# Inputs of four units loaded at once, moves of the first block on ScalarE's queue, and idle products on TensorE: one change to a fused attention and two-layer kernel

## The chip, the cores and the metric

One core of a Trainium2 chip runs the whole program. The metric is the device time of one execution in microseconds (us). One execution was profiled; its span (first to last instruction) and its own time are given below.

## What is computed

The reference, cut to what matters (B, H, S, D = 4, 8, 768, 48; 3072 tokens of 384 numbers; the hidden layers are 2048 wide):

```python
f = 1.0 / (1.0 + np.exp(-f_logit))
for t in range(S):
    state = f[:, :, t, :, None] * state + np.einsum('bhd,bhe->bhde', k[:, :, t], v[:, :, t])
    y[:, :, t] = np.einsum('bhd,bhde->bhe', q[:, :, t], state)
x = y as (3072, 384)
h = x @ w_in;  x = softplus(h) @ w_out            # first layer
h = x @ w_in2; x = (a clipped square of h) @ w_out2   # second layer
```

The weights of the layers arrive as 64-bit floats, everything else as 32-bit floats.

## The kernel before

**Units.** The recurrence is cut into 24 units (4 batches by 6 chunks of 128 time steps); a unit has all 8 heads. `pre(n)` makes a unit ready. It loads four inputs (`t_f`, `t_k`, `t_q` of 256 KB each and `vz` of 192 KB, L536 ff.). ScalarE takes an exponential (L559) and VectorE or ScalarE adds one (L413 or L415); GpSimd writes the first column of `cap` (L563); VectorE runs the scan that gives the running product `ip` (L565). The keys are multiplied by `ip` (L557), ScalarE takes a logarithm and an exponential (L571, L572), and three more passes of VectorE (L557, L575, L557) make the inverse `pt` exact and multiply the queries by it. TensorE transposes the keys (L586) and a copy brings them to `ks`.

`main(n)` then does the unit's products: keys by queries into two banks (`amm`, L605), two masks on VectorE (L611), the update of the state (`dmm`, L631, with L660 and L663 on VectorE), and the output (`ymm`, L646 and, from the second chunk on, L652). ScalarE copies the output from its bank to `ys` (L675), and six transfers per unit (`moves`, issued at L424) put it into the layout that the layers read: `xr2` for the first block, `xhl` for the later ones.

**Layers.** Tokens are taken in six blocks of 512 per layer, and each block in 16 steps of 128 hidden columns. A step is a product `hmm` (L728), the activation on ScalarE and VectorE (L758 to L773), and a product `second` (L807 in the first block, L802 to L804 later). The first block needs four units, since 4 x 128 = 512 tokens. It uses 32-bit products with weights just converted from 64 bits (three VectorE passes, L473, L476, L478, then a transfer `wl<-wa`); chunks 2 to 15 of these weights are converted while the first block runs.

**What sets the order.** The program writes the operations down in one order; `Order.schedule` (a planner with a cost in ns for each operation) then fixes the order on every engine. Engines run their own list strictly in that order and wait on semaphores. Every transfer takes the next of eight completion semaphores in turn, and is issued only when the transfer that had this semaphore before it has landed. Before, all transfers are issued by SP, in one list. Around the start the text writes `pre(0)`, `pre(1)`, the conversion of two weight chunks, `main(0)`, `main(1)`, and then `attention()`, which interleaves `pre(2)`, `main(2)` with `pre(3)`, and so on. There are three buffers of each input, one `ip` and one `pt`, so the fourth unit's inputs go into the first unit's buffers:

```python
t_f = buf("t_f", [P, NA, P], 3, pool=attp)
t_k = buf("t_k", [P, NA, P], NQ, pool=attp)      # NQ = 3
ip = attp.tile([P, NA, P], F32, name="ip")
pt = attp.tile([P, NA, P], F32, name="pt")
```

In orders below, t_f_138 to 140, t_k_141 to 143, t_q_144 to 146 and vz_135 to 137 are the three buffers of each input; stg, wa, wl are the stages of a weight chunk (staged, converted, stored); bank_69 to 76 are the eight banks; ys_156 and 157 the two output buffers; xr_124 is `xr2`; g_127 to 129 are `g_0`, the three buffers of the first block's activation, tu_121 is `t_u`, ip_147 and 148 the two buffers of `ip`.

Of the kernel before, what the change touches and what calls it, by code (L numbers as in the profile page):

```python
# [30 lines left out]
NQ = 3  # L31
# [283 lines left out]
def attn_moe_moe2_kernel(ctx: ExitStack, tc: tile.TileContext, q, k, v, f_logit,  # L315
# [46 lines left out]
    bank = buf("bank", [P, 512], 8, pool=psum)  # L362

# [26 lines left out]
    ip = attp.tile([P, NA, P], F32, name="ip")  # L390
    pt = attp.tile([P, NA, P], F32, name="pt")
# [6 lines left out]

    nc.scalar.preload_act_table_set("natural_log_exp_and_others")
# [122 lines left out]

    abank = [0]
# [11 lines left out]

    def load(n):  # L536


        b, c = divmod(n, NCH)
        t = slice(c * P, c * P + P)  # L540
        dma(t_f[n % 3], f_logit[b, :, :, t], [], [("t_f", n % 3)], 262e3)
        dma(t_k[n % NQ], k[b, :, :, t], [], [("t_k", n % NQ)], 262e3)
        dma(t_q[n % NQ], q[b, :, :, t], [], [("t_q", n % NQ)], 262e3)
        dma(vz[n % NQ], v[b, t], [], [("vz", n % NQ)], 197e3)
        attn_keys.update([("t_f", n % 3), ("t_k", n % NQ), ("t_q", n % NQ), ("vz", n % NQ)])

    def pre(n):
        b, c = divmod(n, NCH)
        z = n % 2
        F, K, Q = t_f[n % 3], t_k[n % NQ], t_q[n % NQ]  # L550
        ktf, kk, kq = [("t_f", n % 3)], ("t_k", n % NQ), ("t_q", n % NQ)
        kip, kpt = [("ip",)], [("pt",)]
# [3 lines left out]
        def tt(o, x, y, op, reads, writes):  # L556
# [9 lines left out]
            out=ip.rearrange("p a t -> p (a t)"), data0=F.rearrange("p a t -> p (a t)"),  # L566
            data1=cap.rearrange("p a t -> p (a t)"), initial=1.0, op0=ALU.mult, op1=ALU.min), ktf + [("cap",)], kip)
        yield
        tt(K, K, ip, ALU.mult, [kk] + kip, [kk])

        ado("act", c_act(NB), lambda: nc.scalar.activation(out=pt, in_=ip, func=AF.Ln), kip, kpt)  # L571
        ado("act", c_act(NB), lambda: nc.scalar.activation(out=F, in_=pt, func=AF.Exp, scale=-1.0), kpt, ktf)  # L572
        yield
        tt(pt, ip, F, ALU.mult, kip + ktf, kpt)
        ado("dve", c_dve(NB), lambda: nc.vector.scalar_tensor_tensor(  # L575
            out=pt, in0=pt, scalar=2.0, in1=F, op0=ALU.subtract, op1=ALU.mult, reverse0=True), kpt + ktf, kpt)
        tt(Q, Q, pt, ALU.mult, [kq] + kpt, [kq])
        ado("dve", c_dve(NA), lambda: nc.vector.tensor_copy(pcall[:, n, :], pt[:, :, P - 1]), kpt, [("pcall", n)])
        yield
        if c < NCH - 1:  # L580
# [7 lines left out]
            ado("pe", 400, f, [kk], [kb])  # L588
            ado(copy_any(NA * R, lambda: ks[z], lambda: pbv, True), 0, None, [kb], [("ks", z)])
# [128 lines left out]


    O1 = [0, 1, 2]  # L720
    H1 = [3, 4]
    H2 = [3, 5, 1]
    O2 = [4, 7, 6]

# [302 lines left out]
```

## Time and profile before

| | |
|---|---|
| time, median of 3 runs (lowest, highest) | 961.5 us (961.21, 963.16) |
| the profiled execution: its own time / its span | 960.75 / 958.7 us |
| TensorE busy | 923.1 us (96%) |
| VectorE, ScalarE, GpSimd busy | 661.4, 641.0, 78.3 us |
| TensorE busy in us 0 to 10, 10 to 20, 40 to 50 of the span | 0.98, 7.00, 3.64 us |
| first block's products run on from | 49.22 us after the start |

How to read it: the profile is one execution; times in its views are us from the span's start. "Busy" is the time an engine executes; a wait is put down to what ended it. SPq is the issuing of transfers by SP, PEclk is TensorE's granted clock as a share of 2.4 GHz.

### The profile page before, as it was taken

The numbers are of one execution on the slowest core, as the hardware profiler recorded it, in microseconds if no ns is written. First come the engines' busy times: TensorE is split into PE (matmuls) and PEld (weight loads), VectorE is DVE, ScalarE is ACT, GpSimd is POOL, SyncE is SP. The second block draws the span as 40 slices with busy tenths as digits, with TensorE's granted clock in tenths as the row PEclk, the third lists the DMA queues.
The fourth block names the chain that finished last, engine by engine and source line by source line (L and its number), as shares of the span: only waits on it lengthen the run. The fifth ranks groups of instructions, "written<-read, shape, count | busy, mean of one in ns | idle before, by whom it ended". The sixth has DMA issues, their size and how long they took to land.

```text
span 958.7 us, 13366 instructions
## 1 busy us (share of the span) xinstructions
PE 923.1 (96%) x4850; PEld 715.7 (75%) x4850; DVE 661.4 (69%) x1034; ACT 641.0 (67%) x1140; POOL 78.3 (8%) x89
## 2 busy tenths in 40 slices
PE   4789998999999999999999999999999999999997
PEld 3544455887787787888887878887888888888885
DVE  5769997998777778756799995444454454544542
ACT  4256656977877787766787777878984454544443
POOL 1001111021001001001003001000010010100000
PEclk9889999999999999999999999999999999999999
DMA  7477856325312322120152356775640100100001
GB/s 215 109 228 237 251 160 204 119 65 175 114 50 75 105 71 71 47 87 17 41 171 69 121 176 181 211 202 195 204 160 1 66 0 1 66 1 1 34 0 37
DMA packets 106890, 103.98 MB, mean 108 GB/s; under 512 B 8001, under 2 KB 89921, under 8 KB 106817
## 3 DMA queue, kind: packets, MB, share of 16 engines
q1 hardware_dynamic: 106816, 103.05, 35.6%
q8 instruction: 40, 0.66, 0.3%
q14 instruction: 34, 0.27, 0.1%
HBM read 78.64 MB, written 9.44 MB: 92 GB/s over the span
## 4 chain that ended last, share of the span: by engine, by line
PE 74%; DVE 11%; DMA 5%; ACT 5%; issue 2%; SPq 2%; POOL 0%; DVEq 0%; ACTq 0%
PE bank L728 33%; PE bank L802 10%; PE bank L804 10%; PE bank L803 10%; PE bank L807 4%; PE bank L605 3%; PE bank L646 2%; SPq L424 2%; PE bank L652 2%; DMA stg<-in_moe_w_in_dram 1%; DVE tl L765 1%; DVE te L763 1%; DVE wa L478 1%; DVE tl L771 1%; PE bank L631 1%
## 5 line engine op out<-in xcount | busy, mean ns | idle before, releaser
L728 PE MATMUL bank<-xhl,wh 128*128 128x512 f32 x840 | 260.4, 391 | 0.0
L728 PEld LDWEIGHTS bank<-xhl,wh 128*128 128x128 f32 x840 | 158.5, 189 | 32.5
L728 PE MATMUL bank<-xhl,wl 128*128 128x512 f32 x420 | 168.3, 401 | 3.0 <-DVE tl L765 3.0
L802 PE MATMUL bank<-gh,wl 128*128 128x512 f32 x420 | 164.6, 392 | 1.0 <-ACT gh L419 1.0
L804 PE MATMUL bank<-gl,wh 128*128 128x512 f32 x420 | 163.9, 390 | 1.4 <-DVE gl L773 1.4
L803 PE MATMUL bank<-gh,wh 128*128 128x512 f32 x420 | 163.5, 389 | 0.0
L419 ACT CAST gh<-tl 128x512 fp32r<-128x512 f32 x176 | 108.9, 619 | 74.4 <-DVE tl L788 48.9
L788 DVE TENSOR_TENSOR tl<-bank,te 128x512 f32<-128x512 f32 x96 | 66.4, 691 | 69.8 <-ACT te L787 69.8
L790 DVE TENSOR_TENSOR gl<-tl,gh 128x512 fp32r<-128x512 f32 x96 | 67.5, 703 | 60.4 <-ACT gh L419 59.5
L758 ACT ACTIVATE te<-bank 128x512 f32<-128x512 f32 x96 | 57.0, 594 | 74.8 <-PE bank L728 74.6
L728 PEld LDWEIGHTS bank<-xhl,wl 128*128 128x128 f32 x420 | 79.2, 189 | 22.8 <-DVE tl L765 4.0
L804 PEld LDWEIGHTS bank<-gl,wh 128*128 128x128 f32 x420 | 78.8, 188 | 19.1 <-DVE gl L773 2.5
L802 PEld LDWEIGHTS bank<-gh,wl 128*128 128x128 f32 x420 | 78.8, 188 | 18.7 <-ACT gh L419 1.8
L803 PEld LDWEIGHTS bank<-gh,wh 128*128 128x128 f32 x420 | 78.9, 188 | 16.2
L783 ACT ACTIVATE te<-bank 128x512 f32<-128x512 f32 x96 | 57.1, 595 | 49.0 <-PE bank L728 48.2
L787 ACT ACTIVATE te<-te 128x512 f32<-128x512 f32 x96 | 60.5, 630 | 40.8 <-DVE te L785 40.8
L763 DVE SCALAR_TENSOR_TENSOR te<-tu,te 128x512 f32<-128x512 f32 x96 | 67.2, 700 | 24.1 <-ACT tu L415 23.8
L785 DVE TENSOR_SCALAR te<-te 128x512 f32<-128x512 f32 x96 | 45.2, 471 | 51.8 <-ACT te L783 51.8
L773 DVE TENSOR_TENSOR gl<-tl,gh 128x512 fp32r<-128x512 f32 x80 | 56.8, 709 | 21.0 <-ACT gh L419 20.6
L765 DVE SCALAR_TENSOR_TENSOR tl<-bank,tl 128x512 f32<-128x512 f32 x96 | 65.8, 685 | 2.2 <-ACT tl L761 2.1
L728 PE MATMUL bank<-xhl,wxh 128*128 128x512 f32 x216 | 66.9, 391 | 0.0
L759 ACT ACTIVATE te<-te 128x512 f32<-128x512 f32 x96 | 60.6, 632 | 2.0
(87 smaller groups left out, 1390.8 us busy)
## 6 DMA issues: line engine op xcount, KB each, us to landing
stg<-in_moe_w_out_dram SPq DMA_DIRECT2D x64, 384.0 KB, 3.9
stg<-in_moe_w_in_dram SPq DMA_DIRECT2D x32, 384.0 KB, 3.7
stg<-in_moe_w_in_dram SPq DMA_DIRECT2D x32, 288.0 KB, 4.1
t_f<-in_f_logit_dram SPq DMA_DIRECT2D x24, 256.0 KB, 3.5
t_k<-in_k_dram SPq DMA_DIRECT2D x24, 256.0 KB, 3.7
t_q<-in_q_dram SPq DMA_DIRECT2D x24, 256.0 KB, 3.8
xhl<-ys SPq DMA_DIRECT2D x80, 72.0 KB, 2.3
wl<-wa SPq DMA_DIRECT2D x14, 384.0 KB, 3.0
```

The source lines that it names most:

```text
L419: "act": (c_act(n, ps), lambda: nc.scalar.copy(o(), x()))}
L728: nc.tensor.matmul(o, l, r, start=(j == 0), stop=(j == n - 1))
L759: do("act", c_act(N), lambda: nc.scalar.activation(out=e, in_=e, func=AF.Exp, scale=-1.0), [ke], [ke])
L763: do("dve", c_dve(N), lambda: nc.vector.scalar_tensor_tensor(out=e, in0=u, scalar=-1.0, in1=e, op0=ALU.add, op1=ALU.subtract), [ku, ke], [ke])
L765: do("dve", c_dve(N), lambda: nc.vector.scalar_tensor_tensor(out=l, in0=h, scalar=0.0, in1=l, op0=ALU.max, op1=ALU.add), [kb, kl], [kl])
L783: do("act", c_act(N, True), lambda: nc.scalar.activation(out=r, in_=h, func=AF.Relu, scale=0.5, bias=0.5), [kb], [kr])
L787: do("act", c_act(N), lambda: nc.scalar.activation(out=r, in_=r, func=AF.Square), [kr], [kr])
L788: do("dve", c_dve(N), lambda: nc.vector.tensor_tensor(out=l, in0=h, in1=r, op=ALU.max), [kb, kr], [kl])
L790: do("dve", c_dve(N), lambda: nc.vector.tensor_tensor(out=gl, in0=l, in1=gh.bitcast(F32), op=ALU.subtract), [kl, kgh], [kgl])
L802: nc.tensor.matmul(o, ol, gh, start=(c == 0), stop=False)
L803: nc.tensor.matmul(o, oh, gh, start=False, stop=False)
L804: nc.tensor.matmul(o, oh, gl, start=False, stop=(c == NFC - 1))
```

## The change

1. All inputs of units 0 to 3 get places of their own: unit 3's go into buffers that the first block uses only later (`g_0` and `t_u`, by `inputs_of`). `ip` gets two buffers and `pt` is gone (the steps that used it work in place in `ip` and `t_f`). The text now writes the first four steps of `pre(0)` to `pre(3)` ahead of everything else; the last step of each and `main(0)`, `main(1)` follow the conversion of two weight chunks, and `attention()` starts with `main(2)`.
2. The six moves of a unit of the first block are issued on ScalarE's queue (`nc.scalar.dma_start`, L717) and no longer on SP's. Later blocks keep SP.
3. TensorE multiplies a zeroed 128x128 tile by itself (`keep_warm`, L532): 18 times at the very start, 5 times after the first unit's transposes, and 5 times after the keys-by-queries products of each of the first four units. Nothing reads the results; they go to a bank that the first block overwrites.

The core of the diff:

```diff
@@ -387,8 +391,7 @@
     t_f = buf("t_f", [P, NA, P], 3, pool=attp)
     t_k = buf("t_k", [P, NA, P], NQ, pool=attp)
     t_q = buf("t_q", [P, NA, P], NQ, pool=attp)
-    ip = attp.tile([P, NA, P], F32, name="ip")
-    pt = attp.tile([P, NA, P], F32, name="pt")
+    ip = buf("ip", [P, NA, P], 2, pool=attp)
     ks = buf("ks", [P, NA, R], 2, pool=attp)
     am = buf("am", [P, NA, P], 2, pool=attp)
     sst = buf("sst", [P, NA, D], 2, pool=attp)
@@ -396,6 +399,8 @@
 
     ys = buf("ys", [P, 2, NA, P], 2, pool=attp)
 
+    warm = attp.tile([P, P], F32, name="warm")
+    nc.vector.memset(warm, 0.0)
     nc.scalar.preload_act_table_set("natural_log_exp_and_others")
 
 
@@ -520,6 +525,14 @@
         attn_keys.update(writes)
         do(eng, cost, fn, reads, writes, delay)
 
+    def keep_warm(n, after=()):
+
+        def f():
+            for _ in range(n):
+                nc.tensor.matmul(bank[H1[1]][:, 0:P], warm, warm, start=True, stop=True)
+
+        do("pe", 217 * n, f, after, [("bank", H1[1])])
+
     abank = [0]
     tbank = [0]
     ndone = [0]
@@ -533,23 +546,32 @@
         abank[0] += 1
         return bank[r], ("bank", r)
 
+    def inputs_of(n):
+
+
+        if n == 3:
+            g = [x.rearrange("p (a t) -> p a t", a=NA) for x in g_0]
+            return (g[2], g[0], g[1], t_u[0][:, 0:NA * E2]), (("gh", 2), ("gh", 0), ("gh", 1), ("tu", 0))
+        i = n if n < 3 else (n - 1) % NQ
+        return (t_f[i], t_k[i], t_q[i], vz[i]), (("t_f", i), ("t_k", i), ("t_q", i), ("vz", i))
+
     def load(n):
 
 
         b, c = divmod(n, NCH)
         t = slice(c * P, c * P + P)
-        dma(t_f[n % 3], f_logit[b, :, :, t], [], [("t_f", n % 3)], 262e3)
-        dma(t_k[n % NQ], k[b, :, :, t], [], [("t_k", n % NQ)], 262e3)
-        dma(t_q[n % NQ], q[b, :, :, t], [], [("t_q", n % NQ)], 262e3)
-        dma(vz[n % NQ], v[b, t], [], [("vz", n % NQ)], 197e3)
-        attn_keys.update([("t_f", n % 3), ("t_k", n % NQ), ("t_q", n % NQ), ("vz", n % NQ)])
+        tiles, keys = inputs_of(n)
+        for o, i, key, size in zip(tiles, (f_logit[b, :, :, t], k[b, :, :, t], q[b, :, :, t], v[b, t]), keys,
+                                   (262e3, 262e3, 262e3, 197e3)):
+            dma(o, i, [], [key], size)
+        attn_keys.update(keys)
 
     def pre(n):
         b, c = divmod(n, NCH)
         z = n % 2
-        F, K, Q = t_f[n % 3], t_k[n % NQ], t_q[n % NQ]
-        ktf, kk, kq = [("t_f", n % 3)], ("t_k", n % NQ), ("t_q", n % NQ)
-        kip, kpt = [("ip",)], [("pt",)]
+        (F, K, Q, _), (kf, kk, kq, _) = inputs_of(n)
+        I = ip[z]
+        ktf, kip = [kf], [("ip", z)]
         load(n)
         yield
 
@@ -563,19 +585,19 @@
         ado("pool", 450, lambda: nc.gpsimd.tensor_scalar(
             out=cap[:, :, 0:1], in0=F[:, :, 0:1], scalar1=2.0 ** 62, scalar2=1.0, op0=ALU.min, op1=ALU.max), ktf, [("cap",)])
         ado("dve", 70 + 2.08 * NB, lambda: nc.vector.tensor_tensor_scan(
-            out=ip.rearrange("p a t -> p (a t)"), data0=F.rearrange("p a t -> p (a t)"),
+            out=I.rearrange("p a t -> p (a t)"), data0=F.rearrange("p a t -> p (a t)"),
             data1=cap.rearrange("p a t -> p (a t)"), initial=1.0, op0=ALU.mult, op1=ALU.min), ktf + [("cap",)], kip)
         yield
-        tt(K, K, ip, ALU.mult, [kk] + kip, [kk])
-
-        ado("act", c_act(NB), lambda: nc.scalar.activation(out=pt, in_=ip, func=AF.Ln), kip, kpt)
-        ado("act", c_act(NB), lambda: nc.scalar.activation(out=F, in_=pt, func=AF.Exp, scale=-1.0), kpt, ktf)
+        tt(K, K, I, ALU.mult, [kk] + kip, [kk])
+
+        ado("act", c_act(NB), lambda: nc.scalar.activation(out=F, in_=I, func=AF.Ln), kip, ktf)
+        ado("act", c_act(NB), lambda: nc.scalar.activation(out=F, in_=F, func=AF.Exp, scale=-1.0), ktf, ktf)
         yield
-        tt(pt, ip, F, ALU.mult, kip + ktf, kpt)
+        tt(I, I, F, ALU.mult, kip + ktf, kip)
         ado("dve", c_dve(NB), lambda: nc.vector.scalar_tensor_tensor(
-            out=pt, in0=pt, scalar=2.0, in1=F, op0=ALU.subtract, op1=ALU.mult, reverse0=True), kpt + ktf, kpt)
-        tt(Q, Q, pt, ALU.mult, [kq] + kpt, [kq])
-        ado("dve", c_dve(NA), lambda: nc.vector.tensor_copy(pcall[:, n, :], pt[:, :, P - 1]), kpt, [("pcall", n)])
+            out=I, in0=I, scalar=2.0, in1=F, op0=ALU.subtract, op1=ALU.mult, reverse0=True), kip + ktf, kip)
+        tt(Q, Q, I, ALU.mult, [kq] + kip, [kq])
+        ado("dve", c_dve(NA), lambda: nc.vector.tensor_copy(pcall[:, n, :], I[:, :, P - 1]), kip, [("pcall", n)])
         yield
         if c < NCH - 1:
             pb, kb = att_bank(n * P < BLOCKS1[0])
@@ -586,15 +608,16 @@
                     nc.tensor.transpose(pbv[:, a, :], K[0:R, a, :], ident[0:R, 0:R])
 
             ado("pe", 400, f, [kk], [kb])
+            if n == 0:
+                keep_warm(5, [kb])
             ado(copy_any(NA * R, lambda: ks[z], lambda: pbv, True), 0, None, [kb], [("ks", z)])
         yield
 
     def main(n):
         b, c = divmod(n, NCH)
         z = n % 2
-        kk, kq = ("t_k", n % NQ), ("t_q", n % NQ)
-        kv = [("vz", n % NQ)]
-        K, Q, V = t_k[n % NQ], t_q[n % NQ], vz[n % NQ]
+        (_, K, Q, V), (_, kk, kq, kv) = inputs_of(n)
+        kv = [kv]
         banks = [att_bank() for _ in range(2)]
 
         def amm():
@@ -604,7 +627,9 @@
                     r = slice(64 * hh, 64 * hh + D)
                     nc.tensor.matmul(banks[hh][0][:, a * P:(a + 1) * P], K[r, a, :], Q[r, a, :], start=True, stop=True)
 
-        ado("pe", 1000, amm, [kk, kq], [kp for _, kp in banks])
+        ado("pe", 1030, amm, [kk, kq], [kp for _, kp in banks])
+        if n < 4:
+            keep_warm(5, [kp for _, kp in banks])
         for hh, (pa, kp) in enumerate(banks):
             pav = pa.rearrange("p (a t) -> p a t", a=NA)
             attn_keys.update([kp, ("am", hh)])
@@ -689,7 +714,8 @@
                     o, i = xr2[dst, 0:3, sl], Y[src, 0, 0:3, :]
                 else:
                     o, i = xr2[dst, m, sl], Y[src, 0, 3, :]
-                dma(o, i, [kyh], [("x0", xs, u)], size)
+                do("act", 500, lambda o=o, i=i: nc.scalar.dma_start(out=o, in_=i), [kyh], [("x0", xs, u)],
+                   delay=1700 + size / 250)
             else:
                 if m is None:
                     for j in range(2):
@@ -703,11 +729,8 @@
 
     def attention():
         done = object()
-        p = pre(2)
-        while next(p, done) is not done:
-            yield 1
         for n in range(2, NU):
-            p = pre(n + 1) if n + 1 < NU else iter(())
+            p = pre(n + 1) if 3 < n + 1 < NU else iter(())
             m = main(n)
             while True:
                 x = next(m, done)
@@ -886,16 +905,23 @@
         t0 += N
 
     s_of = {}
-    for n in range(2):
-        for _ in pre(n):
-            pass
-        s_of[1, n] = load_w(1, n)
+
+    keep_warm(18)
+    first = [pre(n) for n in range(4)]
+    for n, p in enumerate(first):
+        for _ in range(4):
+            next(p)
+        if n < 2:
+            s_of[1, n] = load_w(1, n)
     for c in range(2):
         conv_w(1, c, s_of.pop((1, c)))
         s_of[1, c + 2] = load_w(1, c + 2)
-    for n in range(2):
-        for _ in main(n):
+    for n in range(4):
+        for _ in first[n]:
             pass
+        if n > 0 and n < 3:
+            for _ in main(n - 1):
+                pass
     agen = attention()
     pieces = [0]
 
```

**SP's list** around the first units' outputs. Before (the row "xr_124<-ys_156 48x3x128 x2" is the first two moves of unit 0):

```order
L424 DMA vz_135<-in_v_dram 128x384
L424 DMA xr_124<-ys_156 48x3x128 x2
L424 DMA stg_112<-in_moe_w_in_dram 96x3x256
L424 DMA xr_124<-ys_156 32x128 x2
L424 DMA xr_124<-ys_156 16x128 x2
L424 DMA xr_124<-ys_157 48x3x128 x2
L424 DMA xr_124<-ys_157 32x128 x2
L424 DMA xr_124<-ys_157 16x128 x2
L424 DMA stg_112<-in_moe_w_in_dram 32x3x256
L424 DMA stg_112<-in_moe_w_out_dram 128x768
L424 DMA t_f_139<-in_f_logit_dram 128x4x128
L424 DMA wl_95<-wa_125 128x384 x2
```

Now:

```order
L429 DMA g_129<-in_f_logit_dram 128x4x128
L429 DMA vz_136<-in_v_dram 128x384
L429 DMA t_q_146<-in_q_dram 128x4x128
L429 DMA g_127<-in_k_dram 128x4x128
L429 DMA vz_137<-in_v_dram 128x384
L429 DMA g_128<-in_q_dram 128x4x128
L429 DMA stg_111<-in_moe_w_out_dram 128x768
L429 DMA stg_111<-in_moe_w_in_dram 96x3x256
L429 DMA stg_111<-in_moe_w_in_dram 32x3x256
L429 DMA tu_121<-in_v_dram 128x384
L429 DMA stg_112<-in_moe_w_in_dram 96x3x256
L429 DMA stg_112<-in_moe_w_in_dram 32x3x256
```

The moves have left SP's list: weight chunk 1 (stg_112) and the next two units' inputs no longer stand behind the moves of units 0 and 1, and unit 3's inputs (g_129, g_127, g_128, tu_121) stand ahead of it.

**ScalarE's list** at the outputs of units 2 and 3 (L675 before, L700 now, ys_156 and ys_157). Before:

```order
L419 COPY ks_150<-bank_70 128x448
L675 COPY ys_156<-bank_76 112x512
L559 ACTIVATE t_f_139<-t_f_139 128x512
L415 ACTIVATE t_f_139<-t_f_139 128x512
L675 COPY ys_157<-bank_74 112x512
L419 CAST wh_79<-wl_95 128x768
L571 ACTIVATE pt<-ip 128x512
L572 ACTIVATE t_f_139<-pt 128x512
```

Now, with what each row waits for (DMAHW0 to 7 are the eight completion semaphores of transfers):

```order
L581 ACTIVATE t_f_139<-t_f_139 128x512
L420 ACTIVATE t_f_139<-t_f_139 128x512 [waits Activation_49]
L700 COPY ys_157<-bank_74 112x512 [waits DMAHW3_49,DMAHW1_49,DMAHW6_49,DVE_49,PE_49]
L593 ACTIVATE t_f_138<-ip_147 128x512 [waits DVE_49]
L717 DMA xr_124<-ys_157 48x3x128 [waits DMAHW5_49,Activation_49]
L717 DMA xr_124<-ys_157 48x3x128 [waits DMAHW6_49]
L717 DMA xr_124<-ys_157 32x128 [waits DMAHW0_49]
L717 DMA xr_124<-ys_157 32x128 [waits DMAHW1_49]
L717 DMA xr_124<-ys_157 16x128 [waits DMAHW3_49]
L717 DMA xr_124<-ys_157 16x128 [waits DMAHW4_49]
L594 ACTIVATE t_f_138<-t_f_138 128x512 [waits Activation_49]
L593 ACTIVATE t_f_139<-ip_148 128x512 [waits DVE_49]
```

Between unit 3's output copy and the next work of ScalarE now stand one logarithm of unit 4 and six issues of moves; each of the issues waits for an earlier transfer on its semaphore.

**TensorE's list** at its start, with the idle products (warm); t_k_141 are the keys of unit 0, and L656 is its state update:

```order
L532 MATMUL bank_73<-warm 128x128 x18
L608 MATMUL bank_70<-ident,t_k_141 128x112 x4
L532 MATMUL bank_73<-warm 128x128 x5
L656 MATMUL bank_76<-vz_135,ks_149 64x48
L656 MATMUL bank_76<-vz_135,ks_149 48x48
```

Before, the list began with the transposes of t_k_141.

## Rows read from the trace of the kernel before

**Rows 1.** Busy time by stretch: stretch, length, then each engine's busy us (instructions), PEclk, DMA share, GB/s.

```profile
49.00:60.00 11.00, 9.49 (x17) 4.05 (x18) 5.25 (x9) 5.69 (x9) 0.00 (x0) 0.81 0.84 239
60.00:100.00 40.00, 40.00 (x151) 18.86 (x150) 39.13 (x56) 25.90 (x43) 4.59 (x3) 1.00 0.78 238
100.00:155.00 55.00, 52.24 (x281) 26.53 (x279) 50.63 (x76) 34.42 (x59) 6.35 (x7) 1.00 0.64 187
580.00:952.00 372.00, 371.51 (x1633) 305.54 (x1631) 181.54 (x295) 228.64 (x425) 19.34 (x13) 1.00 0.27 83
```

**Rows 2.** The chain that ended last, us 39 to 61: start, us, what.

```profile
40.86 0.59 ACT ys L675
...
41.48 0.58 SPq L424
...
46.55 0.59 SPq L424
...
47.19 1.79 DMA xr<-ys
...
49.22 3.77 PE bank L728 x4
...
59.01 1.29 PE bank L728 x3
```

**Rows 3.** Timeline of TensorE, products of units 2 and 3: start, us, what, [idle before].

```profile
28.46 2.08 PE L605 MATMUL bank<-t_q,t_k 48*128 48x128 f32 x16
...
36.20 1.16 PE L605 MATMUL bank<-t_q,t_k 48*128 48x128 f32 x16
...
39.74 1.08 PE L652 MATMUL bank<-t_q,sst 48*48 48x128 f32 x16
```

**Rows 4.** Busy time by stretch, as in Rows 1: the clock's fall and rise.

```profile
43.00:44.00 1.00, 0.00 (x0) 0.00 (x0) 0.03 (x1) 0.85 (x2) 0.00 (x0) 0.50 0.69 150
53.00:54.00 1.00, 1.00 (x3) 0.43 (x3) 0.00 (x0) 0.96 (x2) 0.00 (x0) 0.88 1.05 295
```

**Rows 5.** Who held up SP's list, us 0 to 60: waiter, releaser: us in total, times, longest.

```profile
SPq L424 <- ACT pt L571: 5.4, 2, 4.7
```

**Rows 6.** The page's bandwidth by slice of 24 us.

```profile
GB/s 215 109 228 237 251 160 204 119 65 175 114 50 75 105 71 71 47 87 17 41 171 69 121 176 181 211 202 195 204 160 1 66 0 1 66 1 1 34 0 37
```

**Rows 7.** Timeline of VectorE: its first pass of a unit, and the masks of units 2 and 3.

```profile
4.78 0.43 DVE L413 TENSOR_SCALAR t_f<-t_f 128x512 f32<-128x512 f32 x1 [3.30 <-ACT t_f L559]
...
31.05 1.28 DVE L611 TENSOR_TENSOR am<-bank,mask 128x512 f32<-128x512 f32 x2
...
37.39 1.29 DVE L611 TENSOR_TENSOR am<-bank,mask 128x512 f32<-128x512 f32 x2 [1.51 <-PE bank L605]
```

**Rows 8.** Groups by line and shape, us 0 to 45, VectorE: busy us, mean ns | idle before.

```profile
L565 DVE TENSOR_TENSOR_SCAN ip<-t_f,cap 128x512 f32<-128x512 f32 x5 | 6.1, 1217 | 0.0
L611 DVE TENSOR_TENSOR am<-bank,mask 128x512 f32<-128x512 f32 x8 | 5.3, 685 | 4.0 <-PE bank L605 4.0
...
L476 DVE SCALAR_TENSOR_TENSOR wa<-stg,wa 128x384 int32<-128x384 int32 x4 | 2.2, 550 | 0.0
...
L473 DVE TENSOR_SCALAR wa<-stg 128x384 int32<-128x384 int32 x4 | 1.4, 354 | 0.1
...
L578 DVE COPY pcall<-pt 128x4 f32<-128x4 f32 x4 | 0.7, 163 | 0.0
```

**Rows 9.** The same for ScalarE.

```profile
L571 ACT ACTIVATE pt<-ip 128x512 f32<-128x512 f32 x5 | 3.2, 631 | 4.5 <-DVE pcall L578 2.5 <-DVE ip L565 2.0
```

**Rows 10.** Transfers issued in us 35 to 38.5: KB each, us from issue to landing.

```profile
stg<-in_moe_w_out_dram SPq DMA_DIRECT2D x1, 384.0 KB, 6.4
...
xr<-ys SPq DMA_DIRECT2D x1, 72.0 KB, 5.7
```

**Rows 11.** The same, us 38.5 to 48.

```profile
xr<-ys SPq DMA_DIRECT2D x4, 8.0 KB, 1.7
```

**Rows 12.** The page's section of transfers, whole execution: x count, KB each, us to landing.

```profile
stg<-in_moe_w_out_dram SPq DMA_DIRECT2D x64, 384.0 KB, 3.9
```

More of the change, by code (lines that the diff above doesn't have):

```diff
@@ L362, in attn_moe_moe2_kernel @@
     bank = buf("bank", [P, 512], 8, pool=psum)
+    O1 = [0, 1, 2]
+    H1 = [3, 4]
+    H2 = [3, 5, 1]
+    O2 = [4, 7, 6]
     xhl = const.tile([P, 2, NK, XR], F32R, name="xhl")
@@ L653, in ymm @@
                                          start=False, stop=(a == NA - 1))
-        ado("pe", 1900 if c else 1000, ymm, kv + [("am", 0), ("am", 1), kq] + ([k1] if c else []), [ky])
+        ado("pe", (2000 if c else 1070), ymm, kv + [("am", 0), ("am", 1), kq] + ([k1] if c else []), [ky])
         if c < NCH - 1:
@@ L717, in attention @@
                 yield 1
[L720 to L723, printed above, removed]
     def mm3(o, pairs):
@@ L931, in attn_moe_moe2_kernel @@
                 ahead = t0 + N * (c + 1) / NFC
-                attn_upto(5 + (ahead + max(0, ahead - TB) * (RATE - 1)) * 5 / P, t0 + N, t0)
+                attn_upto((ahead + max(0, ahead - TB) * (RATE - 1)) * 5 / P, t0 + N, t0)
                 xk = [(x, s, u) for x in (("xh", "xl") if bi else ("x0",))
@@ L962, in attn_moe_moe2_kernel @@
             released = True
-            held = sorted((x for x in attn_keys if x[0] not in ("bank", "xh", "xl", "xr2", "te", "tl")), key=str)
+            held = sorted((x for x in attn_keys if x[0] not in ("bank", "xh", "xl", "xr2", "x0", "te", "tl", "tu", "gh")), key=str)
             do("none", 0, release, held, [("w2x",), ("acc",)] + held)
```

## The prediction

> **What bounds the kernel now.** I read the busy times by stretch first. From 580 us on TensorE is busy 371.51 of 372 us, and from 60 to 100 without a gap [rows 1]: time is to be had only before the end of the first block at about 155 us. There the idle of TensorE is 11.00 - 9.49 = 1.5 us in 49 to 60 and 55.00 - 52.24 = 2.8 us in 100 to 155 [rows 1], and the large rest lies ahead of 49.22, where the first block's products start to run on [rows 2].
>
> Next the chain. It leaves TensorE at 39.74 + 1.08 = 40.82 [rows 3], passes unit 3's output copy (0.59), then nine issues of SP from 41.48 to 47.14, one every 0.63, then the last move's landing (1.79), and reaches the first block's product at 49.22 [rows 2]. From the copy's end to that product it is 49.22 - 41.45 = 7.8 us.
>
> Ahead of that the timeline of TensorE. The keys-by-queries products of unit 2 take 2.08 us at 28.46, those of unit 3 take 1.16 at 36.20 [rows 3]. So until about 36 us TensorE ran at the lower of its two levels (1.2 GHz) and then at 2.4, although the clock's column reads 1.00 for both: its record begins with the first change, a fall to 0.50 at 43.0, after products had ended at 40.82; it rises again within 53 to 54, after products had run on from 49.22 [rows 2 to 4]. A unit takes 36.20 - 28.46 = 7.7 us, nearly all of it products one behind the other: from unit 1 on TensorE, at the lower level, sets the pace.
>
> Last, SP's waits: the load into unit 0's buffer stood 4.7 us for ScalarE's logarithm [rows 5], and everything behind it stood too.
>
> **The change part by part.**
>
> *Products.* With 18 idle products at the start I take TensorE to be at 2.4 GHz when unit 0's products come. A record of 512 columns takes 1.29 / 3 = 0.43 us at 2.4 GHz and 3.77 / 4 = 0.94 at 1.2 [rows 2]; an idle product is two records of a quarter of that, 0.215 or 0.47 us. The 18 cost 3.9 to 8.5 us in a stretch where TensorE has nothing to do; at 8.5 they may push unit 0's transposes by about 1 us, which VectorE's list hides. Five cost 1.1 us and stand behind the keys-by-queries products, while VectorE runs two masks of 1.28 [rows 7]: hidden at 2.4 GHz. Without that cover each costs what it takes.
>
> *Preparation.* At the higher level VectorE sets the pace. Its list holds 46 passes from its first pass of unit 0 (4.78 before, the same now [rows 7]) to unit 3's second mask: 4 scans of 1.22; 24 full-width passes that follow each other at 0.60 (two masks take 1.28, one 0.685 [rows 7, 8]); 18 short ones (one of 0.43, three of 0.16, nine of 0.35, counting the five state passes like L473, and five of 0.55 [rows 7, 8]), in sum 6.8, less 0.08 each for the overlap, 5.4. That is 4.9 + 14.4 + 5.4 = 24.7, so 29.5 without a wait. Some 1.5 us come on top for the first scans and the first logarithm and exponential (0.63 each [rows 9]), which nothing covers yet: 31.0. The ends: 29.5, and 33.5 if the masks wait as before, 4.0 us [rows 8]. Before it was 37.39 + 1.29 = 38.7 [rows 7].
>
> *Loads.* Unit 3's last input is the fifteenth load, 3.74 MB in; at the 215 GB/s of the first slice [rows 6] it lands about 20 us after the start, and VectorE wants it at about 25. The first 4.7 us of SP's stall are gone; the weights of chunk 1 come early. Gain beyond the sum above: nothing.
>
> *Moves on ScalarE.* No row shows an issue on ScalarE; between nothing and SP's 0.63 I take 0.63, since it is the same instruction, and keep nothing for the range. Unit 2's second mask ends 5.3 us before unit 3's (the 13 passes between), at 25.7; two sets of output products (L646 and L652, 1.08 each, as L652 [rows 3]) and the copy bring 28.5; six issues 3.8, an exponential and an addition 1.3: only at 33.5 is ScalarE free for unit 3's copy, which TensorE has ready at 33.1. Copy 0.6, logarithm 0.63, six issues 3.8, landing 1.8: 40.3. But the last two issues wait on the semaphores of the second half of chunk 1's weights and of a 384 KB stage. These go out only after VectorE's last conversion pass of chunk 1, 2.6 us behind the masks, at 33.6; with two issues of SP the stage starts at 34.8 and lands 3.9 to 6.4 later [rows 10, 12], 38.7 to 41.2. Then 0.6 for the issue, 1.8 for landing and 0.2: the first block starts at 41.3 to 43.8, I take 42.2. Behind these issues stand unit 4's exponential and the conversion of chunk 1's high part, and VectorE's queries of unit 4 wait for the exponential; that is no longer the first block's start. **Gain 49.2 - 42.2 = 7.0 us**, between 5.4 and 7.9, or 9 if an issue is free and no semaphore is late.
>
> Here a rule of the Trainium skill speaks against the change. In this trace a move lands 1.7 to 1.8 us after its issue when little else moves [rows 2, 11], but 5.7 when weights are on the way [rows 10]. "DMA: Bandwidth & Descriptors", section "Issuing engines are not separate DMA queues", says that transfers of all issuing engines run on the same 16 engines and interleave, so that a second queue saves issue time only, which it calls usually small. The nine issues of 0.63 on the chain are not small; by that row the shared engines could cost this change up to 3.9 us: by the rule taken at its word the sum would be the second rival's, by the rows at a quiet time it stays.
>
> *First block.* In the time until the first activation VectorE now has unit 4's keys and queries, unit 5's scan, one high part and one copy behind it (0.6 + 0.6 + 1.1 + 0.5 + 0.5 = 3.3 us more than before). That is backlog it had to work off while busy 39.13 of 40 us [rows 1], so part of TensorE's 4.3 us idle goes: I take 2.5, between 0 and 4.3. The lower level at the block's start stays: TensorE idles from 33 to 42, longer than before; if it doesn't fall, 4 x (0.94 - 0.43) = 2.0 more.
>
> *Sum:* 960.75 (the profiled execution's own time) - 7.0 - 2.5 = **951.2**. The median shown is 0.75 above that execution, less than the least that counts here: about 0.2%, 1.9 us, is what a measurement of this kernel can tell from no change.
>
> **The rivals.**
>
> *More comes back.* Issues on ScalarE are nearly free, the clock doesn't fall, all idle of the block goes: 9 + 4.3 + 1 = 14.3, 946.5. For it: VectorE's idle before the masks. Against: the semaphores above.
>
> *The moves collide with weights.* They are now issued while chunk 3's stage and chunk 1's stores are on the way; 5.7 instead of 1.8 for the last landing [rows 10, 11] is 3.9: 955.1.
>
> *The clock falls between the bursts.* TensorE is idle at times between units 0 and 1; where it falls, a unit takes 7.7 instead of 5.3 us. Twice is 4.8: 956.0.
>
> *Slower: the clock never rises for these products.* Before, products ran nearly without a break from 20 to 36 us at the lower level [rows 3], so it is not certain that idle ones lift it in time. Then TensorE stays the bound, each unit gets five products of 0.47, four bursts 9.4, and unit 3's copy starts at 40.9 + 9.4 = 50.3; copy, logarithm, issues, landing 7.0: 57.3, that is 8.1 later than before, of which the first block's idle can give back 4.3: 964.5. It decides when unit 1's to 3's keys-by-queries products take 2.1 and not 1.1.
>
> *The loads come no earlier.* If four units' inputs run at the 109 GB/s of the second slice [rows 6], the last lands at 37 and the masks are where they were: 960.8.
>
> **How the numbers follow.** The forecast gets 0.50: the chain before is plain, VectorE's list is counted. More comes back 0.16, collision 0.14, clock falling 0.08, clock never rising 0.07, loads late 0.05. Faster by over 0.2% are the first four, 0.88, less 0.01 for their upper tails; slower 0.08; the same 0.05. The range must leave out two in ten at most: 944.5 (the second case with 2 us beyond) to 958.0 (the fourth with 2 us) holds the first four.
>
> **What would show it.** Right: keys-by-queries products of all four units at about 1.1 us; unit 3's second mask ended by about 31 us; ScalarE issuing unit 3's moves from about 35; the first block's products from about 42. Wrong: these products at 2 us, VectorE idle between its passes, moves that land 4 us and more after issue, or a first block that starts at 42 and ends no earlier than 153.

## The result, and the profile after

The changed kernel took **948.04 us** (median of 4 runs, 946.61 to 949.62) against 962.07 us (4 runs, 961.21 to 963.16) before: ratio 0.9854, 95% interval 0.9833 to 0.9875. The forecast was 951.2 with a range of 944.5 to 958.0, so the time lay inside it. The profiled execution took 949.62 us; its span is 947.8. The two profiles differ by 10.9 us in span, the medians by 14.0: the traces show the smaller of the two.

Lines of the changed kernel: keys-by-queries products L628, idle products L532, output copy L700, moves L717, first layer's products L747, SP's loads L429.

Busy times by stretch of the changed kernel, with the columns of [rows 1]; the stretch of the third row is not among [rows 1], and follows for the kernel before:

```profile
49.00:60.00 11.00, 10.46 (x38) 4.92 (x37) 7.86 (x13) 9.05 (x16) 2.13 (x2) 0.98 0.74 228
100.00:155.00 55.00, 55.00 (x325) 30.46 (x324) 49.24 (x74) 36.71 (x64) 8.06 (x9) 1.00 0.68 197
155.00:580.00 425.00, 421.64 (x2491) 340.14 (x2490) 345.36 (x533) 326.75 (x578) 40.18 (x49) 1.00 0.32 96
```

The same stretch in the kernel before:

```profile
155.00:580.00 425.00, 419.54 (x2517) 337.97 (x2516) 351.70 (x540) 328.83 (x576) 44.70 (x53) 1.00 0.33 99
```

TensorE's idle fell from 1.5 to 0.5 us in 49 to 60, from 2.8 to nothing in 100 to 155, and also from 5.5 to 3.4 us behind that, where the longest wait before was this (TensorE's timeline):

```profile
162.66 0.79 PE L728 MATMUL bank<-xhl,wl 128*128 128x512 f32 x1 [2.19 <-DVE tl L765]
```

TensorE's timeline of the changed kernel, with the columns of [rows 3]:

```profile
12.65 1.16 PE L628 MATMUL bank<-t_q,t_k 48*128 48x128 f32 x16 [0.70 <-DVE t_q L579]
...
29.55 1.16 PE L628 MATMUL bank<-g,g 48*128 48x128 f32 x16
...
34.32 1.08 PE L677 MATMUL bank<-g,sst 48*48 48x128 f32 x16
...
45.32 7.46 PE L747 MATMUL bank<-xr,wl 128*128 128x512 f32 x12 [7.38 <-DMA xr<-ys]
```

The keys-by-queries products of units 0 and 3 (and those between) now take 1.16 us, not 2.08 as unit 2's did in [rows 3]. The first block starts at 45.32 instead of 49.22 [rows 2]. The first product that reads `xhl`, the start of the second block, came at 155.0 before and comes at 148.4 now. So the 10.9 us by which the span shrank (958.7 to 947.8) divide into **3.9 ahead of the first block, 2.7 within it (105.8 to 103.1 us), and 4.3 behind it (803.7 to 799.4)**. The borders are starts of products, not equal work: before, two products of the first block ran ahead of 49.22 (at 45.97), and by the start of the second block the changed kernel had done the keys-by-queries products of nine units, the kernel before of eight. So each part is good to one or two us.

What stands before that start: ScalarE's timeline of the changed kernel (ACTq is its issuing of moves):

```profile
25.50 5.04 ACTq L717 DMA_DIRECT2D xr<-ys  x6
...
32.21 0.57 ACT L700 COPY ys<-bank 112x512 f32<-112x512 f32 x1
32.81 4.97 ACTq L717 DMA_DIRECT2D xr<-ys  x6
37.83 0.63 ACT L581 ACTIVATE t_f<-t_f 128x512 f32<-128x512 f32 x1 [5.04 <-DMA xr<-ys]
38.49 0.63 ACT L420 ACTIVATE t_f<-t_f 128x512 f32<-128x512 f32 x1
39.02 0.57 ACT L700 COPY ys<-bank 112x512 f32<-112x512 f32 x1
39.49 0.63 ACT L593 ACTIVATE t_f<-ip 128x512 f32<-128x512 f32 x1
39.62 4.15 ACTq L717 DMA_DIRECT2D xr<-ys  x6
```

and the last step of the chain of waits ahead of the first block's products (start, us, what):

```profile
41.63 3.71 DMA xr<-ys
```

Unit 3's products ended at 34.32 + 1.08 = 35.40, but its copy starts at 39.02: ScalarE stood 5.0 us in unit 2's moves, and before that as long in unit 1's. The landing of 3.71 us that ends the chain is that of the fourth of unit 3's six moves, issued at 41.63; the issues run on to 39.62 + 4.15 = 43.77. Landings of the smallest moves issued in us 38.5 to 48, the last two of the six (KB each, us from issue to landing):

```profile
xr<-ys ACTq DMA_DIRECT2D x2, 8.0 KB, 2.9
```

Such moves took 1.7 us before [rows 11].

### The profile page after: what moved, and what is told of

The parts are those of the page before. It is cut to its first block, busy times and chain, and to the rows that moved or that the text cites. A ratio compares the mean times of both kernels' runs of the same rounds, so it can differ in the third digit from the quotient of the medians.

```text
span 947.8 us, 13531 instructions
## 1 busy us (share of the span) xinstructions
PE 922.9 (97%) x4936; PEld 720.0 (76%) x4936; DVE 655.7 (69%) x1032; ACT 640.3 (68%) x1143; POOL 76.8 (8%) x91
## 4 chain that ended last, share of the span: by engine, by line
PE 88%; DMA 3%; DVE 3%; ACT 2%; SPq 1%; issue 1%; ACTq 0%; POOL 0%; DVEq 0%
PE bank L747 41%; PE bank L821 13%; PE bank L822 12%; PE bank L823 12%; PE bank L826 3%; PE bank L628 2%; PE bank L671 2%; PE bank L677 1%; SPq L429 1%; DMA t_k<-in_k_dram 1%; DMA stg<-in_moe_w_in_dram 1%; PE bank L656 1%; DMA xr<-ys 1%; DMA g<-in_k_dram 1%; DVE wa L481 1%
## 5 line engine op out<-in xcount | busy, mean ns | idle before, releaser
L747 PE MATMUL bank<-xhl,wh 128*128 128x512 f32 x840 | 260.6, 392 | 0.0
L747 PEld LDWEIGHTS bank<-xhl,wh 128*128 128x128 f32 x840 | 158.4, 189 | 32.4
L747 PE MATMUL bank<-xhl,wl 128*128 128x512 f32 x420 | 167.9, 400 | 3.4 <-DVE tl L784 3.4
L822 PE MATMUL bank<-gh,wh 128*128 128x512 f32 x420 | 163.6, 389 | 0.0
L747 PEld LDWEIGHTS bank<-xhl,wl 128*128 128x128 f32 x420 | 79.1, 188 | 23.6 <-DVE tl L784 4.2
L806 ACT ACTIVATE te<-te 128x512 f32<-128x512 f32 x96 | 60.6, 631 | 41.5 <-DVE te L804 41.5
L747 PE MATMUL bank<-xhl,wxh 128*128 128x512 f32 x216 | 67.0, 391 | 0.0
L420 ACT ACTIVATE tu<-te 128x512 f32<-128x512 f32 x96 | 60.5, 630 | 2.1 <-DVE te L782 0.2
```

The source lines that it names most:

```text
L420: "act": (c_act(n), lambda: nc.scalar.activation(out=o, in_=x, func=AF.Identity, bias=1.0))}
L747: nc.tensor.matmul(o, l, r, start=(j == 0), stop=(j == n - 1))
L806: do("act", c_act(N), lambda: nc.scalar.activation(out=r, in_=r, func=AF.Square), [kr], [kr])
L822: nc.tensor.matmul(o, oh, gh, start=False, stop=False)
```

## The experiments

All times are compared with runs of the kernel before beside them (medians 959.9 to 960.9). The changed kernel itself was measured beside a kernel before of 962.07, 2 us more than theirs, so where it is compared with a run, the ratios count beside the times. "First block" and "second block" are the starts of their products in the profiled execution (of e2 and e3 the start from which they run on; two products ran some 3 us ahead of it). By the start of the second block not every kernel has done the same number of units ahead, so that column alone is no measure of what was gained.

| run | what it is | us | ratio (95%) | first block | second block |
|---|---|---|---|---|---|
| - | the changed kernel: inputs, moves, idle products | 948.04 | 0.9854 (0.9833 to 0.9875) | 45.32 | 148.4 |
| e1 | inputs, moves | 964.51 | 1.0047 (1.0028 to 1.0066) | 48.61 | 163.0 |
| e2 | inputs, idle products | 955.37 | 0.9939 (0.9918 to 0.9960) | 43.52 | 150.3 |
| e3 | idle products alone | 958.62 | 0.9976 (0.9959 to 0.9992) | 44.00 | 150.5 |
| e4 | moves alone | 950.81 | 0.9892 (0.9872 to 0.9913) | 48.49 | 151.6 |
| e5 | all, inputs of units 4, 5 late | 963.82 | 1.0040 (1.0017 to 1.0063) | 43.83 | 158.6 |
| e6 | all, idle products planned only | 951.99 | 0.9922 (0.9891 to 0.9953) | 46.11 | 149.6 |
| e7 | idle products, moves | 963.43 | 1.0050 (1.0025 to 1.0075) | 49.62 | 163.6 |
| e8 | all, moves on GpSimd | 947.14 | 0.9867 (0.9838 to 0.9895) | 41.95 | 141.2 |
| e9 | e1, five units' masks on VectorE | 951.85 | 0.9912 (0.9887 to 0.9936) | 48.10 | 153.7 |
| e10 | e2, inputs of units 4, 5 by GpSimd | 950.49 | 0.9888 (0.9862 to 0.9915) | 49.92 | 141.1 |
| e11 | e8, TensorE kept busy to the first block | **942.71** | 0.9815 (0.9799 to 0.9832) | 42.54 | 139.4 |
| e12 | e11, five units' masks on VectorE | 944.84 | 0.9842 (0.9814 to 0.9870) | 42.18 | 141.1 |

**The parts, e1 to e4.** e1 is the changed kernel without idle products, e2 with the moves on SP:

```diff
 # e1
-    keep_warm(18)
-                keep_warm(5, [kb])
-            keep_warm(5, [kp for _, kp in banks])
 # e2 (e4: the other way round, in the kernel before)
-                do("act", 500, lambda o=o, i=i: nc.scalar.dma_start(out=o, in_=i), [kyh], ...)
+                dma(o, i, [kyh], [("x0", xs, u)], size)
```

e3 and e4 add the idle products or the moves alone to the kernel before.

> The changed kernel without any idle product (loads and moves as changed). Theory C (the clock is the main part): keys-by-queries products of units 0 to 2 are back at about 2.1 us instead of 1.16, unit 3's output copy is 3 to 5 us later than at 39.0, and the time is 952 to 956, so 4 to 8 above the changed kernel's 948. Theory L (the early loads and the freed SP are the main part, VectorE sets the pace at either level): 948 to 950.

> The changed kernel with the moves of the first block back on SP (loads and idle products as changed). Theory M (taking the moves off SP is a main part, since weights stand behind them there): 953 to 958. Rival, from the changed kernel's trace, where unit 3's copy waits until 39.0 behind unit 2's moves on ScalarE although its products end at 35.4: ScalarE's queue costs about as much as SP's did, the copy comes at about 36, the first block starts at 41 to 44 instead of 45.3, and the time is 946 to 950.

> The kernel before with only the idle products added (18, 5 and four times 5). Theory C: keys-by-queries products of all units at 1.16, the first block starts at 43 to 45 instead of 49.2, time 953 to 957. Theory L: with three buffers and one ip the units still wait for each other, the first block starts at 48 to 49, time 960 to 962.

> The kernel before with only the moves of the first block on ScalarE's queue. Theory M: the nine issues of SP leave the chain and weights come earlier, 955 to 958. Theory C: products stay at the lower level to about 36 us and set the pace; what SP no longer issues ScalarE does; 959 to 963.

The parts do not add. e2 came out where the theory of the moves had it, e3 between two theories; e1 and e4 missed every theory. The moves alone gave three quarters of the whole gain (1.1 of 1.5%), and with the inputs, but without idle products, they made the kernel slower than before. And the place was wrong: with the moves on SP (e2) the first block starts earlier, at 43.52, than in the changed kernel. TensorE's timeline of e2, where all but two of the first products run from 43.52:

```profile
40.48 2.04 PE L746 MATMUL bank<-xr,wl 128*128 128x512 f32 x2 [7.68 <-DMA xr<-ys]
43.52 6.02 PE L746 MATMUL bank<-xr,wl 128*128 128x512 f32 x10 [1.00 <-DMA xr<-ys]
```

e3 says the same: its block starts 5.2 us sooner than before, and its time falls by 1.6. So what the moves give must lie behind the first product. I looked at what stands behind them in SP's list. SP's timeline of the kernel before, the four inputs of unit 4:

```profile
34.24 0.61 SPq L424 DMA_DIRECT2D t_f<-in_f_logit_dram  x1
...
53.37 0.61 SPq L424 DMA_DIRECT2D t_k<-in_k_dram  x1
...
63.14 0.60 SPq L424 DMA_DIRECT2D t_q<-in_q_dram  x1
...
68.09 0.43 SPq L424 DMA_DIRECT2D vz<-in_v_dram  x1
```

and of the changed kernel, the same four:

```profile
21.22 0.55 SPq L429 DMA_DIRECT2D t_f<-in_f_logit_dram  x1
22.92 0.55 SPq L429 DMA_DIRECT2D t_k<-in_k_dram  x1
24.46 0.54 SPq L429 DMA_DIRECT2D t_q<-in_q_dram  x1
25.10 0.61 SPq L429 DMA_DIRECT2D vz<-in_v_dram  x1
```

Unit 4's keys, queries and values now leave 30 to 43 us earlier, while TensorE still waits for the first block. In e4 they leave at 23.3 to 28.2, in e2 only at 48.6 to 68.1. Hence a new theory: VectorE and ScalarE work ahead on units 4 and 5, and that backlog is missing later. Summed by stretches up to 155 us, the two were busy 211.0 us in the kernel before (VectorE 128.2, ScalarE 82.8), 214.0 in e2 and 225.2 in the changed kernel (133.5 and 91.7).

**Late and early inputs, e5 and e10.** e5 moves these inputs behind the moves in the planner's list (what leaves SP in the freed place, at 20.9 to 29.3 us, is by the edit a later unit's); e10 leaves the moves on SP and lets GpSimd issue these inputs:

```diff
 # e5
-            dma(o, i, [], [key], size)
+            dma(o, i, [("x0", n - 2, u) for u in range(6)] if n in (4, 5) else [], [key], size)
 # e10, beside e2's moves
+            if n in (4, 5):
+                do("pool", 500, lambda o=o, i=i: nc.gpsimd.dma_start(out=o, in_=i), [], [key], ...)
```

> The changed kernel with one thing more: in SP's list the inputs of units 4 and 5 stand behind the moves of units 2 and 3 (by their place in the order; nothing else is meant to change). In the changed kernel unit 4's inputs leave at 21.2 to 25.7 us and unit 5's first at 25.9; with the moves on SP they leave at 48.6 to 68. Theory V (the gain behind the first product comes from these early inputs, with which VectorE and ScalarE work ahead before the block): the first block still starts at 43 to 47, but lasts 106 to 107 us instead of 103.1, and TensorE waits some 2 us again where the second block starts, after which its clock falls: 953 to 957. Rival S (it is the way from unit 3's copy to the first product that matters, or the weights): 946.5 to 950, as the changed kernel.

> The changed kernel with the moves back on SP (955.37 so), and the inputs of units 4 and 5 issued by GpSimd, which has nothing else to do there. Theory V (moving the moves pays because SP then comes early to the inputs of units 4 and 5): the inputs leave at 20 to 30 us though SP has the moves; the first block starts at 43 to 45 as with the moves on SP, lasts 102 to 104 instead of 106.8, and the time is 945 to 950. Rival S (it pays because of what else SP has behind the moves, the weights): 954 to 957.

In e5 unit 4's inputs left at 45.25 to 63.02. The whole gain went, and more than the theory had: ScalarE still issued the moves, the first block even started earlier, and the kernel took 963.82; VectorE and ScalarE had been busy 212.4 us by 155. In e10 they left at 12 to 24 us, the two had been busy 219.4 us, and the kernel with the moves on SP fell from 955.37 to 950.49, just outside what the theory expected (945 to 950); here the planner put products of units 4 and 5 ahead of the block, which starts only at 49.92, but the second block starts 9 us sooner than in e2. So e10 bears out that the early inputs are a part of what the moves on ScalarE gave: it regains 4.9 of the 7.3 us between e2 and the changed kernel, though with another order.

e5 does not settle it. e1 is as slow as e5, and its unit 4's inputs leave as early as the changed kernel's. SP's timeline of e1:

```profile
20.89 0.55 SPq L427 DMA_DIRECT2D t_f<-in_f_logit_dram  x1
...
25.72 0.35 SPq L427 DMA_DIRECT2D vz<-in_v_dram  x1
```

What e1 and e5 share is a wait of TensorE for GpSimd's masks that ends at 112 to 114 us, of which below. Ahead of that wait e5 had not fallen behind e9, which has early inputs, no such wait, and takes 951.85. Busy times by stretch of e5 and of e9:

```profile
0.00:105.00 105.00, 88.73 (x528) 52.77 (x529) 83.89 (x138) 56.67 (x95) 6.43 (x19) 0.95 0.79 221
0.00:105.00 105.00, 78.95 (x451) 44.85 (x452) 86.78 (x144) 52.98 (x89) 5.59 (x17) 0.92 0.79 218
```

VectorE and ScalarE together were busy 140.6 and 139.8 us by then. So early inputs alone do not give the gain, and how much of e5's loss the late ones cost is open. That nothing else behind the moves counts is not shown either: e10 stays 2.5 us above the changed kernel (0.9888 against 0.9854).

**What the idle products do, e6 and e7.** e6 keeps their place and their 217 ns each in the planner's list and issues none. There are 18 + 5 + 4 x 5 = 43 of them, so 9.3 us are planned, not the 38 and 8.2 us that the expectation counts:

```diff
-            for _ in range(n):
-                nc.tensor.matmul(bank[H1[1]][:, 0:P], warm, warm, start=True, stop=True)
+            pass
```

> The changed kernel in which the idle products keep their place and time in the planner's list (38 products, 217 ns each, 8.2 us), but are not issued: every other instruction stands in the changed kernel's order. Theory C (the products work by the clock that TensorE is granted): keys-by-queries products of units 0 to 3 take 2.1 us again, the first block starts later than 45.3, and the time is that of the run without idle products, 961 to 967. Rival P (what changed is the due times, which the 8.2 us shift, and with them the order): 947 to 951, with the products at the lower level.

> The kernel before with idle products and the moves on ScalarE's queue, but without the four units' inputs at once. Alone the idle products gave 1.6 us (958.62 against 960.18), the moves 9.4 (950.81). Theory A (the parts add, and the inputs at once give the small rest): 949 to 951. Rival I (idle products only pay where the inputs are there, since otherwise TensorE waits for inputs and not for its clock; they cost here): 951 to 955. Rival N (inputs at once cost rather than give): 944 to 947.

e6's keys-by-queries products of the first units took 2.08 again, those of unit 2 1.16 (TensorE's timeline of e6):

```profile
12.31 2.08 PE L627 MATMUL bank<-t_q,t_k 48*128 48x128 f32 x16
18.58 2.08 PE L627 MATMUL bank<-t_q,t_k 48*128 48x128 f32 x16
24.91 1.16 PE L627 MATMUL bank<-t_q,t_k 48*128 48x128 f32 x16
```

Yet it took 951.99, not 961 to 967. The clock is worth 951.99 - 948.04 = 4.0 us by the times, 6.5 by the ratios (0.9922 - 0.9854, of 960); the larger part, 964.51 - 951.99 = 12.5 us (12.0 by the ratios), comes from the order that the planned 9.3 us make. P is nearer than C; neither had the split. e7 fell outside all three expectations, and slower than either of its parts alone.

**GpSimd's masks, e9 and e12.** The planner may give the masks of later units to GpSimd. In e2, e3 and the kernel before TensorE waits up to 1.4 us for one of them in the first block; in e1, e5 and e7 alone it waits 2.5 us and more at once. GpSimd's timeline of e1, the slow pair (the next one takes 1.94):

```profile
104.31 7.42 POOL L638 TENSOR_SCALAR_AFFINE_SELECT am<-am 128x512 f32<-128x512 f32 x2 [15.79 <-ACT am L637]
```

TensorE's timeline of e1, the wait that follows, and its waits for these masks in us 45 to 155 (us in total, times, longest):

```profile
111.79 1.36 PE L665 MATMUL bank<-am,vz 128*48 128x128 f32 x14 [2.51 <-POOL am L638]
```

```profile
PE bank L665 <- POOL am L638: 4.8, 3, 2.5
```

Busy times by stretch of e1, with the clock in the third column from the end:

```profile
110.00:115.00 5.00, 3.21 (x31) 2.46 (x31) 2.44 (x4) 1.36 (x3) 1.73 (x1) 0.74 0.72 211
115.00:120.00 5.00, 5.00 (x9) 2.18 (x8) 3.50 (x5) 0.63 (x2) 0.00 (x0) 0.57 0.39 95
```

After the wait the clock is at the lower level for most of ten us. e9 is e1, and e12 is e11, with

```diff
-            if n < 4:
+            if n < 9:
                 do("dve", c_dve(NB), masked, [kp], [("am", hh)])
```

> The changed kernel without the idle products (964.51 so), and the masks of units 4 to 8, which the planner may give to ScalarE and GpSimd, always on VectorE. In the three slow runs (no idle products; late inputs; no inputs at once) one pair of GpSimd's masks in the first block took 7.42, 6.46 and 8.75 us instead of some 2, TensorE waited 2.5 to 3.9 us for it, and its clock fell to 0.57 to 0.72 for the next 5 us. Theory G (this wait and the clock after it make most of what these runs lose): no wait for GpSimd before 150 us, no fall of the clock at 110 to 120, 952 to 958. Rival B (VectorE's list is full there, 1.28 us more for each unit makes TensorE wait for it instead): 960 to 967.

e9 gained 12.7 us on e1, a little more than G expected. Its busy times in the same stretches:

```profile
110.00:115.00 5.00, 5.00 (x23) 2.33 (x23) 4.86 (x7) 3.09 (x5) 0.00 (x0) 1.00 0.61 169
115.00:120.00 5.00, 5.00 (x33) 2.73 (x30) 5.00 (x8) 3.11 (x6) 0.00 (x0) 1.00 0.80 241
```

No idle, no fall of the clock. An estimate from these rows: e1's waits come to 4.8 us, and a clock of 0.74 and 0.57 in five us each costs at most 3.5 more, together 8 of the 12.7. e6, which keeps the idle products' place in the plan, has no such wait either. So most of what that place gave seems to be that TensorE waits for no such mask. For e5 and e7 the same wait (3.8 us each, clock 0.72 and 0.66 behind it) is read from their traces; taking it away was not tried there.

**A better queue and a kept clock, e8, e11 and e12.** e8 issues the moves on GpSimd; e11 adds idle products behind the output products of unit 3 and the three groups of products of unit 4 that precede the block, in e8's order:

```diff
 # e8
-                do("act", 500, lambda o=o, i=i: nc.scalar.dma_start(out=o, in_=i), [kyh], ...)
+                do("pool", 500, lambda o=o, i=i: nc.gpsimd.dma_start(out=o, in_=i), [kyh], ...)
 # e11: in ymm of unit 3, and behind the transposes, dmm and amm of unit 4
+            idle(5 if n == 3 else 0)      # 5, 9, 12 if n == 4
```

> The changed kernel with the first block's moves issued by GpSimd (POOL) instead of ScalarE. In the changed kernel ScalarE stands 5.0 us in unit 2's moves, so that unit 3's copy starts at 39.0 although its products ended at 35.4, and VectorE waits 3.1 us for an exponential behind unit 3's moves. Theory Q (ScalarE's in-order list is the cost): unit 3's copy starts at 35.5 to 36.5, the first block at 41 to 43, the time is 943 to 946. Rival G (GpSimd takes 1 us and more for an issue, or the semaphores of the queue are as late there): the first block starts at 44 to 47, 947 to 952.

> The kernel with the moves on GpSimd (947.14), same order, and 31 more idle products behind the products of units 3 and 4 on the way to the first block (5, 5, 9 and 12), which keep TensorE busy until the first block starts. There the first block's first twelve products take 7.68 us, five of 41.95 to 49.6 at the lower level. Theory H (the clock at the block's start bounds): the first twelve take 5.3 to 5.6 us at a clock of 1.0, unit 4's keys-by-queries products 1.16 instead of 2.08, and the time falls by 1.5 to 3: 944 to 945.6. Rival W (VectorE, not TensorE, sets the pace of the block's beginning, or later waits take it back): 946.3 to 948.

> The fastest kernel so far (moves on GpSimd, idle products until the block starts, 942.71) with the masks of units 4 to 8 always on VectorE. There two of GpSimd's masks still took 3.97 us at 102.4, but TensorE waited for none, and it idled 1.5 us between 100 and 155 us. Theory G2 (GpSimd's masks hurt only where TensorE is led to wait for them): nothing is gained, 942 to 944. Rival B (VectorE is full in the first block, and 1.28 us more for each of five units makes TensorE wait): 945 to 949. Rival G3 (each pair of masks on GpSimd also slows VectorE, so taking them off gives time to both): 939 to 941.5.

In e8 ScalarE's list is free: unit 3's copy starts at 33.23, the first block at 41.95, 3.4 us sooner than with ScalarE. But the time hardly moved (0.9867 against 0.9854): the block starts at the lower level. Busy times by stretch of e8:

```profile
40.00:45.00 5.00, 3.29 (x8) 1.52 (x5) 0.92 (x2) 1.81 (x3) 1.54 (x2) 0.50 0.83 259
45.00:50.00 5.00, 5.00 (x17) 2.03 (x17) 0.95 (x2) 2.81 (x5) 0.00 (x0) 0.84 0.38 88
```

and of e11:

```profile
40.00:45.00 5.00, 5.00 (x30) 3.71 (x30) 1.13 (x3) 1.66 (x3) 1.22 (x2) 1.00 0.78 246
45.00:50.00 5.00, 5.00 (x40) 2.79 (x39) 2.71 (x4) 4.53 (x8) 0.00 (x0) 1.00 0.47 108
```

e11's timeline of TensorE:

```profile
39.76 2.94 PE L530 MATMUL bank<-warm 128*128 128x128 f32 x24
42.54 5.34 PE L755 MATMUL bank<-xr,wl 128*128 128x512 f32 x12
```

The first twelve products take 5.34 instead of 7.68 us, as H expected; the time fell by 4.4 us instead of 1.5 to 3. **e11 at 942.71 is the fastest version**, 1.85% below before, and its granted clock over the whole span is 0.999 (0.991 in e8): the fall at 235 to 245 us that e8 has (0.77 and 0.89 in five us each) is gone too. The wait there is 0.74 us at 232.82, where e8's is 1.56 at 236.54. That may be a part of the rest; why TensorE waits less there was not tried. e12 took 944.84, just outside G2's range and B's, and 2.1 us above e11 with intervals that overlap: no gain. So no harm is seen from masks on GpSimd where TensorE doesn't wait for them.

## Why the prediction was right, and where it was not

- **Time and sign right, but the sum was right by compensation, which is luck.** It had 7.0 ahead of the block, 2.5 within it and nothing behind; the trace has 3.9, 2.7 and 4.3. The median, 948.04, is nearer to the rival "more comes back" (946.5) than to the forecast, though two of that rival's conditions failed: the issues on ScalarE were not free, and the clock fell (0.50 in 40 to 45 us).
- *Clock.* TensorE "at 2.4 GHz when unit 0's products come": right, 1.16 us for all four units. Its price by itself is 4.0 to 6.5 us (e6). That the planned time of idle products moves the order was not considered, and is worth two to three times as much.
- *Preparation.* Unit 3's second mask was to end at 31.0; it ended at 32.76 (31.48 + 1.28). Inside the ends.
- *Moves on ScalarE, the step that failed.* An issue took 0.62 to 0.63 us, as assumed, but unit 3's copy started at 39.02 where 33.5 was taken: with their semaphore waits a unit's six moves hold ScalarE 5.0 us, not 3.8, and unit 1's held up unit 2's copy as unit 2's held up unit 3's (32.21, where 28 was taken). From the copy's start to the first product it was 6.3 us, less than the 8.7 taken: the late semaphores that the sum allowed for behind the last issues hardly came (six issues in 4.15 us, against 3.8 without a wait), and the last landings took 2.9, not 1.8. The rival of the colliding moves had named such landings, and the larger moves' 4.1 and 4.7 us were among the signs of being wrong. More basic: the term took the nine issues of SP for the cost to be saved. e2 shows that with everything else changed SP's issues reach the first block by 43.52, sooner than ScalarE's.
- *The Trainium skill's rule* ("DMA: Bandwidth & Descriptors", section "Issuing engines are not separate DMA queues") says that a second queue saves issue time only, usually little. For the way to the first block the trace agrees: 43.52 with SP, 45.32 with ScalarE. But the moves alone gave 1.1% (e4), which the rule doesn't count. They took waiting transfers out of an in-order list; that this is the cause, e10 bears out in part.
- *First block.* 2.5 forecast, 2.7 measured. TensorE's idle in the two stretches fell by 3.7 us, as the mechanism named, VectorE's backlog, would have it. Unit 4's and 5's early inputs, which the text only touched ("VectorE now has unit 4's keys and queries"), are a part of it by e10; that they are all of it is not shown.
- *Behind the first block.* "Time is to be had only before the end of the first block" was wrong. TensorE idled 5.5 us in 155 to 580; one wait there was 2.19 us for VectorE at 162.66, with a clock of 0.75 in 160 to 165. In the changed kernel that wait is 0.55 us; another, of 1.98 us at 240.10, is left.
- *The rival "slower".* It named the clock that never rises. A slower kernel was indeed near (e1, e5, e7 at 963 to 965), but by another way: waits for GpSimd's masks on TensorE's path, shown for e1 by e9 and only read from the traces of e5 and e7.

## What to carry to other kernels

When transfers leave a queue, look first at what stands behind them in that in-order list and when it is needed, then at their own way. Where a planner sets the order, cost a dummy operation twice: once issued, once only planned. And find every stretch in which an otherwise busy engine waits: with the 2.19 us that ended at 162.66 in the kernel before, the clock was 0.75 in 160 to 165 us and 0.91 in 165 to 170, so such a wait can cost more than its own length.

## What the runs showed of the hardware that was not expected

GpSimd's masks of one size (128 x 512) took 0.84 us each in one pair and 4.4 in another. GpSimd's timeline of e7 and of the kernel before:

```profile
110.43 8.75 POOL L637 TENSOR_SCALAR_AFFINE_SELECT am<-am 128x512 f32<-128x512 f32 x2 [26.73 <-ACT am L636]
```

```profile
111.04 1.68 POOL L619 TENSOR_SCALAR_AFFINE_SELECT am<-am 128x512 f32<-128x512 f32 x2 [22.68 <-ACT am L618]
```

In both VectorE works almost without a gap (8.29 of 8.80 us in e7, all of 1.80 in the other). Where the pair is fast, VectorE's passes beside it are longer; its timeline in the kernel before, where this pass takes 1.04 us (0.69 for the same pass at 138.62 in e1):

```profile
111.18 1.04 DVE L763 SCALAR_TENSOR_TENSOR te<-tu,te 128x512 f32<-128x512 f32 x1
```

So one of the two seems to wait for the other. The Trainium skill has a rule of that kind ("SBUF — State Buffer", section "SBUF: two separate sides"): VectorE's passes with two inputs in SBUF (the on-chip memory of the tiles) and GpSimd's that read there take a shared pair of ports in turn, for a whole instruction. These rows agree with it; why GpSimd lost for 7 us in one order and for none in another, no run here shows.

An issue of a move on GpSimd took about 0.55 us (six in 3.24 us in e8), no more than SP's or ScalarE's 0.63.
